# Soft mixture of experts behind attention: the experts' outputs combined as fp32 products on four row groups

## The chip, the cores and the metric

The kernel runs on one core of one Trainium2 chip. A core has five engines that run side by side and wait for each other through semaphores: TensorE (PE in the profile, with its weight loads as PEld), VectorE (DVE), ScalarE (ACT), GpSimd (POOL) and SyncE (SP), which here issues the transfers between DRAM and the on-chip memory SBUF. Products of TensorE land in PSUM, eight banks of 2 KB per partition, and are copied from there to SBUF by ACT or DVE. The metric is the device time of one execution in microseconds; less is better.

## The reference, cut to what matters

Attention with a memory term gives `x` of 4608 rows and 512 columns (eight batches of 576 rows). The change touches what is done with `x` last:

```python
logits = x @ phi                                  # 4608 x 32: 8 experts, 4 slots each
d = exp(logits - max over rows); d /= d.sum(0)    # dispatch
slot_input = (d.T @ x).reshape(8, 4, 512)
for e in range(8):
    slot_out[e] = relu(slot_input[e] @ w1[e]) @ w2[e]
c = exp(logits - max over slots); c /= c.sum(1)   # combine weights
return c @ slot_out                               # 4608 x 32 times 32 x 512
```

## The kernel before

The program has two parts. The first, up to about 464 us, walks over 32 pairs of heads (eight batches, four pairs) and computes attention. As blocks of 512 rows of `x` (nine blocks, `NQ`) are finished, it accumulates the dispatch and prepares the combine weights of blocks 0 to 6. The order of its operations is written out by hand as a list of names (`SEQ`), and a function `pin` ties every instruction to its predecessor on the same engine, so each engine runs in the order of the code. In this part the first 44 of 64 weight tiles of the experts (512 KB each) are loaded by SP into free places of SBUF (`wload`; `wslot` notes the place of each). The change does not touch it.

The second part, from about 464 us on, is the code after `pl.release()`:

- `f1(eg, f)`: first expert layer for a group of four experts and half of the hidden units, as products on four column groups of 32 (one expert each), then relu on ACT. `f1t` transposes the result through PSUM; DVE copies it to `hT`.
- `f2(dh, eg, f)`: second layer for half `dh` of the 512 output columns, also on four column groups. Its sum over `eg` and `f` is in `po[dh]`.
- `c1`, `c2`: the combine weights of blocks 7 and 8, and their transposes, into `cT`. In `cT` partition 32 j + s holds slot s for the j-th run of 128 rows of a block, for j from 0 to 3.
- `reload`: the 20 weight tiles not yet loaded go into the places of tiles that `f1` has read. SP issues them one after another.
- `c3(i, j)`: for each j, from the 32 rows of `cT`, a tile of 96 rows in the reduced type fp32r: the rounded weights, the remainder, and the rounded weights again. Two casts on ACT (`act`, line 355), one subtraction on DVE (line 984). `i` is 0 for blocks 0 to 7 and 1 for block 8.
- `g1(dh)` scales the experts' outputs by the dispatch's denominator on DVE (line 991). `g2(dh)` sums and spreads them to all partitions by a product with the constant `sel` (line 995), and splits them in the same way as the weights: `so` holds the rounded outputs in rows 0 to 63 and the remainder in rows 64 to 95.
- `comb(dh, t4)`: four products of 96 rows, one for each j (line 1006). Their three blocks of rows add up rounded times rounded, remainder times rounded, and rounded times remainder. Two j share a PSUM tile; ACT copies the first pair and DVE the second to SBUF, and SP issues the transfer of 512 x 256 numbers to the output (line 1008).

At the end stands the order: all of `f1`, `c1`, `c2`, `c3` and `f2` for the first half of the columns, `g1(0)`, a quarter of a step of `f2(1, 0, 0)`, `g2(0)`, the rest of that step, five `comb(0, ...)`, `f2(1, 0, 1)`, four more `comb(0, ...)`, the rest of `f2` for the second half, `g1(1)`, `g2(1)`, nine `comb(1, ...)`.

PSUM in this part: `psF` has two buffers of one bank for `f1` and `f2`, `psP` two for `f1t`, `c1`, `c2` and `g2`, `psC` four for `comb`.

Of the kernel before, what the change touches and what calls it, by code (L numbers as in the profile page):

```python
# [8 lines left out]
F32 = mybir.dt.float32  # L9
F32R = mybir.dt.float32r  # L10
AF = mybir.ActivationFunctionType
ALU = mybir.AluOpType
AX = mybir.AxisListType
PSUM = bass.MemoryType.PSUM
# [268 lines left out]
def tile_attn_soft_moe(ctx, tc, q, k, v, M, beta, phi, w1, w2, cst, out):  # L283
    nc = tc.nc
# [8 lines left out]
    cT = const.tile([128, NQ, 128], F32, name="cT")  # L293
# [29 lines left out]
    par = [ctx.enter_context(tc.tile_pool(name=f"par{i}", bufs=1)) for i in range(2)]  # L323
# [30 lines left out]
    def act(o, i):  # L354
        nc.scalar.copy(o, i)  # L355
# [385 lines left out]
    wt, wslot = {}, {}  # L741
# [169 lines left out]
    nw = len(WORD)  # L911
# [4 lines left out]


    psF = ctx.enter_context(tc.tile_pool(name="psF", bufs=2, space=PSUM, reuse_waits="tile"))
    psP = ctx.enter_context(tc.tile_pool(name="psP", bufs=2, space=PSUM, reuse_waits="tile"))
    psC = ctx.enter_context(tc.tile_pool(name="psC", bufs=4, space=PSUM, reuse_waits="tile"))  # L920
    reload = [wslot[order[x]] for x in [*range(8), *range(12, 4 + len(order) - nw)]]
    stage = [wslot[order[x]] for x in range(4 + len(order) - nw, 42)]
    cslot = [wslot[order[x]] for x in range(8, 12)]
    hT = rest[:, 0:2048].rearrange("a (e x y) -> a e x y", e=2, x=8)
    hs, po, cc = {}, {}, {}

# [8 lines left out]
        nc.scalar.activation(h, ps, AF.Relu)  # L935

    def f1t(eg, f):
        pt = psP.tile([128, 512], F32, name="pp")
        for x in range(4):
            nc.tensor.transpose(out=pt[:, 128 * x:128 * x + 128], in_=hs[eg, f][:, 128 * x:128 * x + 128], identity=ident)  # L940
        dve(hT[:, eg, 4 * f:4 * f + 4, :].rearrange("a x y -> a (x y)"), pt)
# [9 lines left out]


    def c1(qd):
        ps = psP.tile([128, 512], F32, name="pp")
        nc.tensor.transpose(out=ps[:, 0:128], in_=y["lt"][:, qd - 7, :], identity=ident)
        lk = ps[:, 0:128].rearrange("a (j s) -> a j s", s=32)
        m4 = sml.tile([128, 4], F32, name="m4")
        nc.vector.reduce_max(out=m4, in_=lk, axis=AX.X)
        c = cc[qd] = sml.tile([128, 4, 32], F32, name=("lt", "ex")[qd - 7], bufs=1)
        nc.vector.tensor_tensor(out=c, in0=lk, in1=m4.rearrange("a (j x) -> a j x", x=1).broadcast_to([128, 4, 32]), op=ALU.subtract)  # L960
        nc.scalar.activation(c, c, AF.Exp)
        s4 = sml.tile([128, 4], F32, name="s4")
        nc.vector.reduce_sum(out=s4, in_=c, axis=AX.X)
        nc.vector.tensor_scalar(out=s4, in0=s4, scalar1=1e-9, scalar2=None, op0=ALU.add)
        nc.vector.reciprocal(out=s4, in_=s4)
        nc.vector.tensor_tensor(out=c, in0=c, in1=s4.rearrange("a (j x) -> a j x", x=1).broadcast_to([128, 4, 32]), op=ALU.mult)

    def c2(qd):
        ps = psP.tile([128, 512], F32, name="pp")
        nc.tensor.transpose(out=ps[:, 0:128], in_=cc[qd].rearrange("a j s -> a (j s)"), identity=ident)  # L970
        act(cT[:, qd, :], ps[:, 0:128])


    cst4, cst8 = [], xkp.tile([128, 4, 128], F32R, name="xk")

    def c3(i, j):
        r = slice(32 * j, 32 * j + 32)
        if i == 0:
            pool, name = cslot[j]
            cst4.append(pool.tile([128, 8, 128], F32R, name=name))  # L980
        o, w = ((cst4[j], cT[r, 0:8]), (cst8[:, j], cT[r, 8]))[i]
        act(o[0:32], w)
        act(o[64:96], w)
        nc.vector.tensor_tensor(out=o[32:64], in0=w, in1=o[64:96].bitcast(F32), op=ALU.subtract)


    so = par[0].tile([128, 2, 256], F32R, name="k")
    ogs = par[1].tile([128, 2, 256], F32, name="k")

    def g1(dh):  # L990
        nc.vector.tensor_scalar(out=ogs[:, dh], in0=po[dh][:, 0:256], scalar1=dt, scalar2=None, op0=ALU.mult)

    def g2(dh):
        pm = psP.tile([128, 512], F32, name="pp")
        nc.tensor.matmul(pm[:, 0:256], sel, ogs[:, dh], start=True, stop=True)
        act(so[0:96, dh], pm[0:96, 0:256])
        nc.vector.tensor_tensor(out=so[64:96, dh], in0=pm[64:96, 0:256], in1=so[64:96, dh].bitcast(F32), op=ALU.subtract)

    def comb(dh, t4):
        pool, name = stage[NQ * dh + t4]  # L1000
        o = pool.tile([128, 4, 256], F32, name=name)
        for half in range(2):
            ps = psC.tile([128, 2, 256], F32, name="pc")
            for v2 in range(2):
                u = 2 * half + v2
                nc.tensor.matmul(ps[:, v2], (cst4[u][0:96, t4, :] if t4 < 8 else cst8[0:96, u, :]), so[0:96, dh], start=True, stop=True)  # L1006
            (act, dve)[half](o[:, 2 * half:2 * half + 2, :], ps)
        nc.sync.dma_start(out=out[512 * t4:512 * t4 + 512, 256 * dh:256 * dh + 256].rearrange("(u a) d -> a u d", a=128), in_=o)

    f1(0, 0)  # L1010
# [7 lines left out]
    c2(8)  # L1018
    f1(1, 1)
    f1t(1, 0)  # L1020
    c3(0, 0)
    f2(0, 0, 0)
    f1t(1, 1)
    for x, (pool, name) in enumerate(reload):
        wload(nw + x, pool, name)
    for j in range(1, 4):
        c3(0, j)
    for j in range(4):
        c3(1, j)
    f2(0, 0, 1)  # L1030
    f2(0, 1, 0)
    f2(0, 1, 1)
# [79 lines left out]
```

## Time and profile before

| what | us |
|---|---|
| median of 3 runs (lowest to highest) | 531.93 (530.93 to 534.14) |
| span of the profiled execution | 529.8 |
| TensorE busy | 462.5 (87%) |
| DVE busy | 384.3 (73%) |
| ACT busy | 342.4 (65%) |
| SP's transfers on the 16 DMA engines | 61.6% of their time |

The profile is of one execution; its span runs from the first to the last instruction, and no device time is given for that execution beside the span. The shares are averages over the whole program. In the profile L12 is line 12 of the kernel; a row such as `pf<-w,at` names the tile written and the tiles read, without buffer numbers. Many tiles of the second part carry the names of places that an earlier tile held (`w`, `xt`, `q`, `K`, `X`, `mv`, `rm`). An fp32 product shows as two records, an fp32r product and a transpose as one. In a row of the timeline the first number is the start in the span, the second the length from the start of the first to the end of the last of its records; in brackets stands the idle time before it and what ended that.

### The profile page before, as it was taken

What the parts mean: (1) busy time and instruction counts of PE and PEld (TensorE: products, weight loads), DVE (VectorE), ACT (ScalarE), POOL (GpSimd) and SP (SyncE); (2) the same over time, 40 slices, a digit from 0 to 9 for tenths busy, and PEclk for the clock granted to TensorE, in tenths of its full rate; (3) what the DMA queues carried; (4) which work ended last, traced back from release to release, by engine and by line L of the source; (5) the groups of instructions that cost most, each with busy time, mean ns of one, the idle gap of its engine ahead of it and who ended that gap; (6) DMA issues with size and microseconds to landing.
All of it is one profiled execution on the core that took longest, in us unless ns stands there. A gap on an engine that the chain in (4) does not pass through costs nothing.

```text
span 529.8 us, 11904 instructions
## 1 busy us (share of the span) xinstructions
PE 462.5 (87%) x3970; PEld 312.9 (59%) x3970; DVE 384.3 (73%) x1324; ACT 342.4 (65%) x985; POOL 126.0 (24%) x138
## 2 busy tenths in 40 slices
PE   8989889789998799899888897999998988989783
PEld 5656566556666566576555665766665655634462
DVE  6889788787697688879767878588886864534442
ACT  5777777666788477757767677676874864316432
POOL 4233122332213214235113332223324200000000
PEclk9999999999999999999989999899998989999795
DMA  5654655766465446554646565374564765999599
GB/s 198 178 143 132 191 158 150 209 191 188 142 200 146 137 136 171 143 147 128 188 123 171 185 182 162 83 233 117 158 203 125 218 196 168 379 415 408 222 337 323
DMA packets 66285, 101.78 MB, mean 192 GB/s; under 512 B 11248, under 2 KB 41520, under 8 KB 66224
## 3 DMA queue, kind: packets, MB, share of 16 engines
q1 hardware_dynamic: 65936, 100.93, 61.6%
q8 instruction: 32, 0.52, 0.4%
q14 instruction: 29, 0.24, 0.2%
q10 hardware_dynamic: 288, 0.09, 0.1%
HBM read 91.25 MB, written 9.73 MB: 191 GB/s over the span
## 4 chain that ended last, share of the span: by engine, by line
PE 36%; DMA 25%; DVE 21%; SPq 6%; ACT 5%; issue 4%; POOL 1%; DVEq 0%; POOLq 0%; ACTq 0%
PE oa L598 6%; PE psT L560 6%; DMA rb<-rd 5%; PE psS L433 5%; DVE q L462 4%; PE psS L427 4%; DMA rm<-rs 4%; DMA k<-in_k_dram 4%; DMA rd<-rq 3%; DVE zq L462 3%; PE pf L932 3%; DVE qp L550 3%; PE pc L1006 3%; PE psT L592 3%; DMA q<-in_M_dram 2%
## 5 line engine op out<-in xcount | busy, mean ns | idle before, releaser
L355 ACT COPY at<-psT 128x256 f32<-128x256 f32 (+1 forms) x202 | 86.5, 479 | 52.3 <-PE psT L560 49.1
L470 ACT ACTIVATE q<-q,nm 128x512 f32<-128x512 f32 (+2 forms) x160 | 97.6, 612 | 15.3 <-DVE nm L462 15.2
L598 PE MATMUL oa<-at,mv 128*64 128x320 f32 (+4 forms) x640 | 93.1, 427 | 3.0 <-DMA mv<-in_v_dram 1.3
L427 PE MATMUL psS<-k,qq 128*128 128x256 f32 (+2 forms) x320 | 69.2, 330 | 16.5 <-DVE nm L462 12.0
L462 DVE CUSTOM_DVE_ANT_0 q<-psS,mv 128x512 f32<-128x512 f32 (+1 forms) x128 | 76.1, 611 | 6.6 <-PE psS L433 3.9
L560 PE MATMUL psT<-cs,q 128*128 128x128 f32 x480 | 75.6, 282 | 2.8 <-DVE xt L633 1.1
L433 PE MATMUL psS<-K,X 64*128 64x512 f32 (+2 forms) x576 | 70.5, 365 | 8.5 <-DVE nm L462 6.1
L470 ACT ACTIVATE zq<-zq,nm 128x256 f32<-128x256 f32 (+2 forms) x128 | 67.7, 531 | 7.2 <-DVE nm L462 6.6
L427 PEld LDWEIGHTS psS<-k,qq 128*128 128x128 f32 x320 | 51.9, 199 | 28.3 <-DVE nm L462 17.6
L560 PEld LDWEIGHTS psT<-cs,q 128*128 128x128 f32 x480 | 58.0, 148 | 9.0 <-issue 2.3
L433 PEld LDWEIGHTS psS<-K,X 64*128 64x128 f32 x576 | 46.1, 188 | 26.9 <-issue 9.8
L598 PEld LDWEIGHTS oa<-at,mv 128*64 128x64 f32 x640 | 38.1, 137 | 38.0 <-issue 27.0
L560 PE MATMUL psT<-cs,zq 128*128 128x128 f32 x288 | 48.5, 283 | 2.3 <-DVE xt L633 0.9
L505 POOL TENSOR_SCALAR qp<-qq 128x576 f32<-128x576 f32 x19 | 31.8, 1676 | 74.0 <-PE psT L593 60.2
L550 DVE TENSOR_TENSOR qp<-qp,rb 128x576 f32<-128x576 f32 x32 | 27.0, 843 | 21.2 <-DMA rb<-rd 21.2
L626 DVE TENSOR_TENSOR xt<-oa,rm 128x448 f32<-128x448 f32 (+7 forms) x60 | 23.8, 435 | 24.2 <-DMA rm<-rs 18.1
L411 POOL TENSOR_TENSOR K<-k,K 128x512 fp32r<-128x512 f32 x25 | 32.8, 1314 | 31.3 <-ACT K L355 18.9
L358 DVE COPY at<-psT 128x512 f32<-128x512 f32 (+1 forms) x59 | 32.4, 570 | 10.1 <-PE psT L560 8.6
L592 PE MATMUL psT<-qp,q 128*128 128x512 f32 x64 | 35.1, 629 | 4.4 <-DVE qp L550 3.1
L560 PEld LDWEIGHTS psT<-cs,zq 128*128 128x128 f32 x288 | 34.8, 147 | 6.1 <-ACT at L355 1.1
L530 POOL TENSOR_TENSOR rn<-rn,rm 128x144 f32<-128x144 f32 x22 | 10.5, 477 | 91.3 <-ACT rn L523 57.9
L470 ACT ACTIVATION_READ_ACCUMULATOR q<-q,nm 128x1 f32 x160 | 31.0, 193 | 0.0
(214 smaller groups left out, 760.7 us busy)
## 6 DMA issues: line engine op xcount, KB each, us to landing
w<-in_w_dram SPq DMA_DIRECT2D x49, 512.0 KB
qq<-in_q_dram SPq DMA_DIRECT2D x32, 480.0 KB
mv<-in_v_dram SPq DMA_DIRECT2D x64, 160.0 KB
k<-in_k_dram SPq DMA_DIRECT2D x32, 288.0 KB
rb<-rd SPq DMA_DIRECT2D x64, 144.0 KB
rm<-rs SPq DMA_DIRECT2D x64, 144.0 KB
q<-in_M_dram SPq DMA_DIRECT2D x32, 80.0 KB
out_dram<-w SPq DMA_DIRECT2D x5, 512.0 KB
```

The source lines that it names most:

```text
L355: nc.scalar.copy(o, i)
L358: nc.vector.tensor_copy(out=o, in_=i)
L411: ALU_ENG[ev("kl", n)].tensor_tensor(out=K2[:, 1, :], in0=st[n]["k"][:, 0:512], in1=K2[:, 0, :].bitcast(F32), op=ALU.subtract)
L427: nc.tensor.matmul(ps[:, c + x0 - k0:c + x1 - k0], s["qd"][:, i], s["k"][:, x0:x1], start=True, stop=True)
L433: nc.tensor.matmul(ps[:, c0:c0 + N], X[ROW[h], x, 128 * i - 128:128 * i], K2[ROW[h], y, 0:N], start=(x, y) == (0, 0), stop=(x, y) == (0, 1))
L462: nc.vector.tensor_tensor_reduce(out=sm, in0=src, in1=msk, op0=ALU.add, op1=ALU.min, scale=-0.125, scalar=m0, accum_out=acc_o)
L470: nc.scalar.activation(sm, sm, AF.Exp, scale=-1.0, bias=s["nm"][:, J:J + 1], accum_out=s["sum"][:, J:J + 1])
L505: ALU_ENG[ev("qmin", n)].tensor_scalar(out=st[n]["qp"], in0=st[n]["q"], scalar1=0.0, scalar2=None, op0=ALU.min)
L550: ALU_ENG[ev("qn", n)].tensor_tensor(out=s["qp"], in0=s["qp"], in1=s["rb"], op=ALU.mult)
L560: nc.tensor.transpose(out=ps[:, 128 * x:128 * x + 128], in_=src[:, k0:k0 + 128], identity=ident)
L592: nc.tensor.matmul(om, s["m"][:, 0:128], s["qp"][:, 64:576], start=True, stop=True)
L598: nc.tensor.matmul(o[ROW[h], col:col + nx], vt[:, c, ROW[h]], at[:, a0 + hs * h:a0 + hs * h + nx], start=start, stop=stop)
```

## The change

`c3` and its tiles are gone. The combine takes `cT` as it is: half `half` and index `v2` of a pair pick the 32 rows of `cT` for j = 2 half + v2, and the product is of fp32 with the same 32 rows of `so`, which now holds the experts' outputs unsplit in all four groups of 32 partitions. The two products of a pair write to two PSUM banks; `psC` is gone, and `psP` has three buffers of two banks each, which `comb` shares with `f1t`, `c1`, `c2` and `g2`. The four places that `c3` took (those of tiles 8 to 11) take reloads, and the list of reloads ends with place 19 instead of 23.

```diff
-    psP = ctx.enter_context(tc.tile_pool(name="psP", bufs=2, space=PSUM, reuse_waits="tile"))
-    psC = ctx.enter_context(tc.tile_pool(name="psC", bufs=4, space=PSUM, reuse_waits="tile"))
-    reload = [wslot[order[x]] for x in [*range(8), *range(12, 4 + len(order) - nw)]]
-    stage = [wslot[order[x]] for x in range(4 + len(order) - nw, 42)]
-    cslot = [wslot[order[x]] for x in range(8, 12)]
+    psP = ctx.enter_context(tc.tile_pool(name="psP", bufs=3, space=PSUM, reuse_waits="tile"))
+    reload = [wslot[order[x]] for x in range(len(order) - nw)]
+    stage = [wslot[order[x]] for x in range(24, 42)]
...
-        ps = psP.tile([128, 512], F32, name="pp")
+        ps = psP.tile([128, 2, 512], F32, name="pp")[:, 0]
...
-    cst4, cst8 = [], xkp.tile([128, 4, 128], F32R, name="xk")
-
-    def c3(i, j):
-        r = slice(32 * j, 32 * j + 32)
-        if i == 0:
-            pool, name = cslot[j]
-            cst4.append(pool.tile([128, 8, 128], F32R, name=name))
-        o, w = ((cst4[j], cT[r, 0:8]), (cst8[:, j], cT[r, 8]))[i]
-        act(o[0:32], w)
-        act(o[64:96], w)
-        nc.vector.tensor_tensor(out=o[32:64], in0=w, in1=o[64:96].bitcast(F32), op=ALU.subtract)
...
-    so = par[0].tile([128, 2, 256], F32R, name="k")
+    so = par[0].tile([128, 2, 256], F32, name="k")
...
-        act(so[0:96, dh], pm[0:96, 0:256])
-        nc.vector.tensor_tensor(out=so[64:96, dh], in0=pm[64:96, 0:256], in1=so[64:96, dh].bitcast(F32), op=ALU.subtract)
+        act(so[:, dh], pm[:, 0:256])
...
-            ps = psC.tile([128, 2, 256], F32, name="pc")
+            ps = psP.tile([128, 2, 512], F32, name="pp")
             for v2 in range(2):
-                u = 2 * half + v2
-                nc.tensor.matmul(ps[:, v2], (cst4[u][0:96, t4, :] if t4 < 8 else cst8[0:96, u, :]), so[0:96, dh], start=True, stop=True)
-            (act, dve)[half](o[:, 2 * half:2 * half + 2, :], ps)
+                r = slice(64 * half + 32 * v2, 64 * half + 32 * v2 + 32)
+                nc.tensor.matmul(ps[:, v2, 0:256], cT[r, t4, :], so[r, dh], start=True, stop=True)
+            (act, dve)[half](o[:, 2 * half:2 * half + 2, :], ps[:, :, 0:256])
...
-    for j in range(1, 4):
-        c3(0, j)
-    for j in range(4):
-        c3(1, j)
```

What stands in a row on DVE between the last copies of `f1t` and the first copies of `comb(0, ...)`, before (`w_6132` to `w_6207` and `xk` are the split weights, `k` the tiles of `g1` and `g2`):

```order
L984 TENSOR_TENSOR w_6132<-cT,w_6132 32x1024
L358 COPY at<-pp 128x512
L984 TENSOR_TENSOR w_6199<-cT,w_6199 32x1024
L984 TENSOR_TENSOR w_6203<-cT,w_6203 32x1024
L984 TENSOR_TENSOR w_6207<-cT,w_6207 32x1024
L984 TENSOR_TENSOR xk<-cT,xk 32x128 x4
L991 TENSOR_SCALAR k<-pf,dt 128x256
L997 TENSOR_TENSOR k<-pp,k 32x256
L358 COPY w_6293<-pc 128x512
```

And now:

```order
L358 COPY at<-pp 128x512 x3
L976 TENSOR_SCALAR k<-pf,dt 128x256
L358 COPY w_6260<-pp 128x512
L358 COPY w_6270<-pp 128x512
L358 COPY K_6280<-pp 128x512
```

Between the last transpose's copy and `g1` no instruction is left, and none between `g1` and the first copy of an output. ACT, at the same place, before:

```order
L355 CAST w_6132<-cT 32x1024 x2
L355 CAST w_6199<-cT 32x1024 x2
L355 CAST w_6203<-cT 32x1024 x2
L355 CAST w_6207<-cT 32x1024 x2
L355 CAST xk<-cT 32x128 x8
L355 CAST k<-pp 96x256
L355 COPY w_6293<-pc 128x512
```

And now:

```order
L355 COPY cT<-pp 128x128 x2
L933 ACTIVATE qp<-pf 128x512
L355 COPY k<-pp 128x256
L355 COPY w_6260<-pp 128x512
L355 COPY w_6270<-pp 128x512
```

The sixteen casts are gone, and the copy of `g2` stands right behind the last relu. On TensorE the number and the order of the products stay. SP's reloads, before (the name after DMA is the place):

```order
L752 DMA w6_6171<-in_w2_dram 128x1024
L752 DMA w7_6173<-in_w2_dram 128x1024
L752 DMA w12_6175<-in_w2_dram 128x1024
L752 DMA w13_6177<-in_w2_dram 128x1024
L752 DMA w14_6179<-in_w2_dram 128x1024
```

And now:

```order
L752 DMA w6_6163<-in_w2_dram 128x1024
L752 DMA w7_6165<-in_w2_dram 128x1024
L752 DMA w8_6167<-in_w2_dram 128x1024
L752 DMA w9_6169<-in_w2_dram 128x1024
L752 DMA w10_6171<-in_w2_dram 128x1024
```

From the ninth reload on each goes to a place that is four lower.

More of the change, by code (lines that the diff above doesn't have):

```diff
@@ L937, in f1t @@
     def f1t(eg, f):
-        pt = psP.tile([128, 512], F32, name="pp")
+        pt = psP.tile([128, 2, 512], F32, name="pp")[:, 0]
         for x in range(4):
@@ L968, in c2 @@
     def c2(qd):
-        ps = psP.tile([128, 512], F32, name="pp")
+        ps = psP.tile([128, 2, 512], F32, name="pp")[:, 0]
         nc.tensor.transpose(out=ps[:, 0:128], in_=cc[qd].rearrange("a j s -> a (j s)"), identity=ident)
         act(cT[:, qd, :], ps[:, 0:128])
-    cst4, cst8 = [], xkp.tile([128, 4, 128], F32R, name="xk")
-    def c3(i, j):
-        r = slice(32 * j, 32 * j + 32)
-        if i == 0:
-            pool, name = cslot[j]
-            cst4.append(pool.tile([128, 8, 128], F32R, name=name))
-        o, w = ((cst4[j], cT[r, 0:8]), (cst8[:, j], cT[r, 8]))[i]
-        act(o[0:32], w)
-        act(o[64:96], w)
-        nc.vector.tensor_tensor(out=o[32:64], in0=w, in1=o[64:96].bitcast(F32), op=ALU.subtract)
-    so = par[0].tile([128, 2, 256], F32R, name="k")
+    so = par[0].tile([128, 2, 256], F32, name="k")
     ogs = par[1].tile([128, 2, 256], F32, name="k")
@@ L993, in g2 @@
     def g2(dh):
-        pm = psP.tile([128, 512], F32, name="pp")
+        pm = psP.tile([128, 2, 512], F32, name="pp")[:, 0]
         nc.tensor.matmul(pm[:, 0:256], sel, ogs[:, dh], start=True, stop=True)
-        act(so[0:96, dh], pm[0:96, 0:256])
-        nc.vector.tensor_tensor(out=so[64:96, dh], in0=pm[64:96, 0:256], in1=so[64:96, dh].bitcast(F32), op=ALU.subtract)
+        act(so[:, dh], pm[:, 0:256])
     def comb(dh, t4):
@@ L1020, in tile_attn_soft_moe @@
     f1t(1, 0)
-    c3(0, 0)
     f2(0, 0, 0)
```

## The prediction

> **What bounds the kernel now.** I read the page for the shares, then the stages of the tail (the change touches nothing earlier), then the chain of waits in the tail, then SP's own rows. First the busy time by stages; the columns are stage, length, busy time of each engine, granted TensorE clock, DMA share, GB/s:
> ```profile
> 464.60:490.30 25.70, 24.63 (x280) 10.65 (x284) 9.40 (x20) 10.99 (x16) 0.00 (x0) 1.00 1.03 413
> 490.30:495.50 5.20, 1.53 (x10) 0.50 (x2) 2.82 (x6) 3.06 (x9) 0.00 (x0) 0.81 0.96 383
> 495.50:501.00 5.50, 5.50 (x39) 3.64 (x38) 1.74 (x4) 1.86 (x4) 0.00 (x0) 0.56 0.06 24
> 501.00:510.60 9.60, 9.24 (x119) 5.83 (x118) 4.62 (x8) 3.57 (x7) 0.00 (x0) 1.00 1.00 337
> 510.60:514.00 3.40, 1.93 (x11) 1.36 (x11) 1.36 (x3) 1.06 (x3) 0.00 (x0) 1.00 1.05 350
> 514.00:516.00 2.00, 2.00 (x9) 1.88 (x10) 1.52 (x3) 1.36 (x3) 0.00 (x0) 0.50 0.83 282
> 516.00:525.00 9.00, 4.88 (x21) 4.35 (x20) 4.15 (x6) 3.12 (x6) 0.00 (x0) 0.50 1.08 378
> 525.00:528.20 3.20, 0.00 (x0) 0.00 (x0) 0.00 (x0) 0.00 (x0) 0.00 (x0) 0.50 0.98 333
> ```
> The DMA engines are full with weight reads until 495.5, nearly idle (24 GB/s) until 501.0, and full with the output until 528.2; only 514 to 516 dips. From 501.0 the output, not TensorE, sets the end. So the hole of 5.5 us is what the change can win, and the chain says who makes it:
> ```profile
> 482.65 0.93 ACT w L355
> ...
> 493.54 0.28 DVE xk L984
> 493.82 0.03 issue
> 493.85 0.49 DVE k L991
> 494.34 0.04 issue
> 494.39 1.22 PE pp L995 x2
> 495.61 2.72 PE pf L949 x24
> 498.33 2.33 PE pc L1006 x10
> ```
> From 482.65 on it is the splitting of the combine weights (c3: ACT's L355 into w and xk, DVE's L984), then g1 (L991), which stands behind c3 on DVE, g2 (L995), a rest of f2 (L949), the first combine (L1006). The same steps ahead of the second combine, and SP's first issue of output:
> ```profile
> 511.15 0.71 PE pp L995 x2
> ...
> 511.89 0.38 ACT k L355
> ...
> 512.77 8.13 PE pc L1006 x36
> ```
> ```profile
> 500.27 1.24 SPq L1008 DMA_DIRECT2D out_dram<-w  x2
> ```
> An issue at 500.27 moves data at 501.0: 0.73 us.
>
> **The change, part by part.** c3 goes:
> ```profile
> L355 ACT CAST w<-cT 32x1024 fp32r<-32x1024 f32 x8 | 8.3, 1041 | 0.1
> L355 ACT CAST xk<-cT 32x128 fp32r<-32x128 f32 x8 | 2.4, 295 | 0.1
> ```
> ```profile
> L984 DVE TENSOR_TENSOR w<-cT,w 32x1024 fp32r<-32x1024 f32 x4 | 4.9, 1215 | 3.4 <-ACT w L355 3.4
> L984 DVE TENSOR_TENSOR xk<-cT,xk 32x128 fp32r<-32x128 f32 x4 | 1.1, 281 | 0.4
> ```
> 10.7 us of ACT and 6.0 of DVE. What is late next is f2(0), ahead of g1 on TensorE:
> ```profile
> 482.69 0.38 PE L949 MATMUL pf<-qq,at 128*32 128x256 f32 x1
> ...
> 482.90 0.38 PE L949 MATMUL pf<-qq,at 128*32 128x256 f32 x1
> ...
> 488.38 2.34 PE L949 MATMUL pf<-w,at 128*32 128x256 f32 x40
> ```
> Four column groups start a round together, a round is 0.216 us and its results are there 0.38 after its start (0.17 past the round); an fp32 product takes two rounds. Of the 40 records 32 (eight rounds) belong to f2(0): the last starts at 488.38 + 7 x 0.216 = 489.89 and ends at 490.27.
>
> The third buffer of psP takes away two waits ahead of that:
> ```profile
> 473.08 0.33 PE L955 MATMUL pp<-cs,rb 128*128 128x128 f32 x1 [0.68 <-DVE at L358]
> ```
> ```profile
> 478.03 0.33 PE L970 MATMUL pp<-cs,ex 128*128 128x128 f32 x1 [0.36 <-ACT cT L355]
> ```
> With three in rotation each finds its buffer free. Bounds 0 and 1.04 us; I take 1.04, since TensorE has no other gap there (24.63 busy of 25.70). f2(0) then ends at 489.23. The weights for it and for f2(1) are earlier: 512 KB at 413 GB/s are 1.27 us, the twenty reloads end at 495.5, so the eighth lands at 480.3.
>
> g1 then ends at 489.23 + 0.04 + 0.48 = 489.75, g2's product (0.71 at full clock) at 490.50, ACT's copy at 490.92; DVE's subtraction (L997) is gone. The rest of f2(1,0,0), six rounds at full clock instead of 2.72 us at half, ends at 490.50 + 1.30 = 491.8. The first combine starts there instead of 498.3.
>
> The new products: per tile of 512 rows four of fp32, two rounds each, on four row groups. The trace has no fp32 product on 32 rows. Bounds: all four side by side, 2 x 0.216 = 0.43 us a tile; one after another, 1.73. Before, it was 8.13/9 = 0.90 at half clock, so the one end is a gain and the other a loss on TensorE. The nearest row is that of two row groups of 64:
> ```profile
> L433 PEld LDWEIGHTS psS<-K,X 64*128 64x128 f32 x12 | 1.0, 184 | 1.2 <-DVE nm L462 1.2
> ```
> ```profile
> 303.58 1.49 PE L433 MATMUL psS<-K,X 64*128 64x384 f32 x12 [0.98 <-DVE nm L462]
> ```
> Twelve loads of 0.184 are 2.2 us, yet they are busy for 1.0: the two row groups load side by side, and all twelve products fit into 1.49. I take 0.43.
>
> The Trainium skill, "TensorE: Matmul & The Clock Gate", section "Part 3: Packing small matmuls — row/col tiling", says that a weight load overlaps running products only in another row group; within one, load and product would alternate. By these rows each group's six loads would take 1.1 us and leave 0.39 of the 1.49 for six products, 0.07 each, a third of a round: the trace disagrees. By that rule a buffer would be held for 2 x (0.186 + 0.216) + 0.89 = 1.69, a tile cost 1.13 at full clock, still under the output's pace, and the sum would stand; at half clock it would not, which is rival B.
>
> With products that short the buffers pace the combine:
> ```profile
> L358 DVE COPY w<-pc 128x512 f32<-128x512 f32 x5 | 3.5, 692 | 4.2 <-PE pc L1006 4.2
> ```
> ```profile
> L355 ACT COPY w<-pc 128x512 f32<-128x512 f32 x5 | 2.9, 587 | 4.5 <-PE pc L1006 4.4
> ```
> A buffer is held for 0.43 + 0.17 + 0.04 + 0.64 (mean of the copies) + 0.04 = 1.32 us; three give a half each 0.44, a tile each 0.88. The output needs 524 KB at 378 GB/s = 1.39 us a tile: hidden, with the copies; without that cover it would cost 18 x 0.88 = 15.8. g2's and f1t's use of the same pool adds no wait, their slots being read out by then.
>
> First output: 491.8 + 0.22 + 0.60 + 0.04 + 0.69 = 493.3. SP issues it behind the last reload, whose data end at 495.5, so output flows from 495.5 instead of 501.0. The reloads now take slots 8 to 11 instead of 20 to 23: freed earlier, but the queue is full anyhow, so nothing either way. The work ahead of 464.6 is untouched.
>
> Second combine: first ten halves 9 x 0.44 + 0.43, to 496.2; f2 eight rounds, 497.9; eight halves, 501.4; sixteen rounds and 0.17, 505.1; g1, g2 and copy 1.65, 506.7; first tile 1.55, issue at 508.3, data at 509.0. Until then nine tiles have to last: before, 9.6 x 337 + 3.4 x 350 = 4425 of 4719 KB by 514.0, the rest in 0.84 at 350: 13.8 us, here until 509.3. Covered with 0.3 us to spare; every later us costs itself.
>
> Sum: the 9.44 MB took 501.0 to 528.2, 27.2 us, of which the dip cost 2.0 x (350 - 282)/350 = 0.4. Without it 495.5 + 26.8 = 522.3, and 1.6 after the last data (528.2 to 529.8 before): 523.9, which is 5.9 below the profiled 529.8. The median of the runs is 531.93, 2.1 above the profiled span; I carry the difference: **526.0**. Bounds: all output at 378 GB/s, 25.0 us, gives 524.2; all at 337 gives 527.2, and a second combine late by 0.8 makes that 528.0.
>
> **The rivals.** (B) The second combine runs at half clock and becomes TensorE's. Rows for half clock (the smaller numbers are at full):
> ```profile
> L995 PEld LDWEIGHTS pp<-k,cs x4: 186/238/333, 494.4 to 511.3; 128*128 128x128 f32 x4
> L995 PE MATMUL pp<-k,cs x4: 379/558/794, 494.4 to 511.5; 128*128 128x256 f32 x4
> ```
> A round doubles to 0.43, results 0.37 later. Side by side a buffer holds 0.85 + 0.37 + 0.72 = 1.94, a tile 1.29: still under 1.39. If load and product of one group alternate, 2 x (0.33 + 0.43) + 0.37 + 0.72 = 2.61, a tile 1.74, nine 15.7: 506.7 + 15.7 = 522.4, plus 0.73 + 1.39 + 1.6 = 526.1, time 528.2. For it: 514 to 525 stood at 0.50 after the pause around g2. Against it: L433. This is also what the skill's rule would give.
>
> (C) The clock falls already in the first combine. 491.8 + 5 x 1.29 + 3.46 + 4 x 1.29 + 6.9 + 2.5 for g1, g2 and copy + 2.4 for a tile = 518.7; data at 519.4, 13.2 us for nine tiles, 1.6: 534.2, time 536.3. For it: the clock fell at 514 and stayed down although TensorE was busy for 2.00 of 2.00 us. Against it: 501.0 to 510.6 stood at 1.00 with products and f2 mixed as here.
>
> (D) Row groups of 32 do not overlap in fp32: 1.73 a tile. The end is then 503.4 + 18P (491.8, f2 5.4, g1 to copy 1.65, last half and landing 4.6), P being a tile's products; above P = 1.47 the kernel is slower than before. 1.73 gives 534.5, time 536.7; with half clock in the second combine 550.1, time 552. For it: no such row exists. Against it: L433's two groups.
>
> **How the numbers follow.** Forecast 0.67, B 0.14, C 0.08, D 0.11. A measurement of this kernel can tell about 1% (5.3 us) from no change: faster than 526.6, slower than 537.3. The forecast's 526.0 lies just beyond, so of its 0.67 I give 0.47 to faster; the rest with B, C and half of D is within 1% (0.47); D with half clock is 0.06. The range goes from the forecast's lower bound, 524.0, past B to no change, 532.0, since a partial overlap puts P anywhere below 1.47; it leaves out C and D, 0.19.
>
> **What would show it.** Right: the copies into fp32r are gone, L976 (g1) starts near 489.3 and the first L992 issue near 493.3; GB/s never falls near zero between 495 and 522; L990's eight products of a tile take under 0.9 us. Wrong: L976 waits on something else than f2; a hole in the DMA rate before the tenth output (B, C); L990 records in single file (D); an output that flows at another rate than 337 to 378 moves the end without TensorE.

## The result, and the profile after

| | before | changed |
|---|---|---|
| median of 20 executions each (lowest to highest), us | 533.89 (529.47 to 541.53) | 531.39 (522.95 to 539.61) |
| ratio changed to before | | 0.987 (95% interval 0.983 to 0.991) |
| span of the profiled execution, us | 529.8 | 529.8 |

The changed kernel is faster by 1.3%, between 0.9 and 1.7%. On the 531.93 us of the prediction that is 525.0 us; 526.0 had been predicted. The ratio is formed from executions in which nothing disturbed the core, so it is not the quotient of the two medians, and the profiled execution of the changed kernel is not one of them.

That execution shows why two equal spans say nothing here. The chain of waits shows where the second part begins, first of before, then of the changed kernel (start, length, engine, tile, line, number of records; rows of "issue" are left out):

```profile
464.64 7.07 PE pf L932 x64
```

```profile
469.69 7.07 PE pf L930 x64
...
488.99 5.36 PE pf L947 x96
494.38 0.50 DVE k L976
494.92 0.70 PE pp L980 x2
495.62 1.43 PE pf L947 x24
497.05 0.66 PE pp L990 x8
497.73 0.59 ACT w L355
498.36 0.73 PE pp L990 x6
499.11 0.70 DVE w L358
499.86 0.72 PE pp L990 x7
...
511.04 0.49 DVE k L976
...
512.73 0.72 PE pp L990 x8
```

The first product of `f1` stands at 464.64 before and at 469.69 now: the part that the change does not touch took 5.05 us longer in this execution. From there to the end it is 529.8 - 464.6 = 65.2 us before and 60.1 now, 5.06 less by the unrounded times. All readings below are therefore from the first product of `f1` on; the stretch from there to the end of the span is called the tail.

The page's busy times follow the code: ACT has 331.8 us (342.4 before), DVE 378.0 (384.3), TensorE 461.3 (462.5).

```profile
PE 461.3 (87%) x4042; PEld 307.6 (58%) x4042; DVE 378.0 (71%) x1314; ACT 331.8 (63%) x969; POOL 124.5 (23%) x138
```

In the chain the splits of the weights are gone: ahead of `g1` (L976) stands `f2` (L947) alone. `g1` starts 24.69 after `f1`, before it was 29.21; the first combine (L990) follows 2.6 later, before 4.4. The busy time by stages, in the columns of the prediction's first view:

```profile
469.69:494.30 24.61, 24.36 (x280) 10.62 (x284) 5.63 (x17) 3.54 (x8) 0.00 (x0) 1.00 1.02 411
494.30:499.30 5.00, 4.57 (x60) 2.44 (x50) 1.36 (x3) 1.47 (x4) 0.00 (x0) 1.00 0.98 391
499.30:512.30 13.00, 11.42 (x150) 6.00 (x146) 5.64 (x9) 3.98 (x7) 0.00 (x0) 1.00 1.02 350
512.30:515.00 2.70, 2.01 (x24) 1.46 (x24) 0.82 (x2) 1.45 (x3) 0.00 (x0) 1.00 0.33 114
515.00:528.10 13.10, 5.56 (x52) 2.86 (x48) 5.17 (x8) 4.09 (x7) 0.00 (x0) 0.78 1.04 360
```

The hole of 5.5 us at 24 GB/s between the last reload and the first output is closed: 391 GB/s and then 350. The clock stays at 1.00 through both combines (the 0.78 of the last row is the time after 522, when TensorE has done). But a new hole has opened, 2.7 us at 114 GB/s. SP's rows show what the transfers wait for there, first of the changed kernel, then the tenth issue of before:

```profile
498.54 1.72 SPq L992 DMA_DIRECT2D out_dram<-w  x2
...
508.48 1.21 SPq L992 DMA_DIRECT2D out_dram<-qq  x1
514.29 0.37 SPq L992 DMA_DIRECT2D out_dram<-w  x1
```

```profile
514.30 0.37 SPq L1008 DMA_DIRECT2D out_dram<-w  x1
```

The ninth issue is at 508.48, the tenth, which is the first of the second combine, at 514.29. By 513.2 (43.5 after `f1`) 99% of the nine tiles are written, and the queue runs dry until the tenth. So the first output goes out 6.8 us sooner than before (28.85 after `f1` instead of 35.64), and the tenth 5.06 sooner (44.60 instead of 49.66). The end follows the tenth: 15.53 behind its issue in both kernels.

### The profile page after: what moved, and what is told of

The parts are those of the page before. It is cut to its first block, busy times and chain, and to the rows that moved or that the text cites. A ratio compares the mean times of both kernels' runs of the same rounds, so it can differ in the third digit from the quotient of the medians.

```text
span 529.8 us, 12019 instructions
## 1 busy us (share of the span) xinstructions
PE 461.3 (87%) x4042; PEld 307.6 (58%) x4042; DVE 378.0 (71%) x1314; ACT 331.8 (63%) x969; POOL 124.5 (23%) x138
## 4 chain that ended last, share of the span: by engine, by line
PE 34%; DMA 24%; DVE 24%; SPq 6%; ACT 4%; issue 4%; POOL 1%; DVEq 0%; POOLq 0%; ACTq 0%
DMA rm<-rs 9%; PE psT L560 6%; DVE q L462 5%; PE psS L427 5%; PE oa L598 4%; PE psS L433 4%; DVE zq L462 3%; DMA q<-in_M_dram 3%; DMA rs<-rts 3%; DMA k<-in_k_dram 3%; PE pf L947 3%; PE pf L930 2%; DVE at L358 2%; PE psT L592 2%; PE pp L990 2%
## 5 line engine op out<-in xcount | busy, mean ns | idle before, releaser
L427 PE MATMUL psS<-k,qq 128*128 128x256 f32 (+2 forms) x320 | 67.7, 324 | 15.3 <-DVE nm L462 12.6
L427 PEld LDWEIGHTS psS<-k,qq 128*128 128x128 f32 x320 | 50.8, 195 | 27.2 <-DVE nm L462 18.2
```

The source lines that it names most:

```text
L427: nc.tensor.matmul(ps[:, c + x0 - k0:c + x1 - k0], s["qd"][:, i], s["k"][:, x0:x1], start=True, stop=True)
```

## The experiments

**What was to be told apart.** The theory is that of the prediction: the gain is the hole, it closes because the splits are off the path to `g1`, with shares for the third buffer and for a clock that no longer falls; then the output's rate sets the end as long as the second combine is ready in time. The rivals: the fast products on four row groups are what counts (D of the prediction, if they do not run side by side); the clock is what counts; the second combine is what sets the end, and with it the way in which `f2` is spread among the first combine.

All positions follow from each profile in one way: the start of the row in question less the start of the first product of `f1` (for the changed kernel 494.38 - 469.69 = 24.69). `g1`, combine, outputs and end are in us after `f1`; the last column is the ratio of the times to before, with its interval.

| run | `f1` starts | `g1` | first combine | first output | tenth output | end (tail) | ratio |
|---|---|---|---|---|---|---|---|
| before | 464.64 | 29.21 | 33.62 | 35.64 | 49.66 | 65.19 | 1 |
| changed | 469.69 | 24.69 | 27.29 | 28.85 | 44.60 | 60.13 | 0.987 (0.983 to 0.991) |
| e1_again | 473.89 | 24.69 | 27.29 | 28.85 | 44.60 | 60.13 | 0.990 (0.986 to 0.995) |
| e11_again5 | 469.80 | 24.69 | 27.29 | 28.85 | 44.61 | 60.13 | 0.992 (0.987 to 0.996) |
| e10_before_again | 469.22 | 30.90 * | 35.31 | 37.33 | 51.45 | 66.88 | |
| e2_splits_kept | 472.17 | 29.87 * | 33.72 | 35.68 | 51.43 | 66.63 | 1.002 (0.997 to 1.007) |
| e3_one_group | 468.06 | 24.68 | 27.29 | 30.07 | 65.96 | 97.15 | 1.058 (1.050 to 1.067) |
| e4_spread | 466.70 | 26.38 * | 28.98 | 30.54 | 44.39 | 60.54 | 0.991 (0.987 to 0.995) |
| e5_before_third_buffer | 467.04 | 28.19 | 32.41 | 33.95 | 48.94 | 64.12 | 0.998 (0.994 to 1.002) |
| e6_before_warm | 464.99 | 29.21 | 31.81 | 33.34 | 47.23 | 62.89 | 0.995 (0.991 to 0.999) |
| e7_moved | 475.17 | 24.69 | 27.29 | 28.85 | 43.40 | 60.40 | 0.988 (0.982 to 0.994) |
| e8_two_buffers | 467.68 | 25.71 | 28.32 | 29.88 | 54.52 | 73.64 | 1.021 (1.015 to 1.026) |
| e9_three_places | 468.91 | 24.69 | 27.29 | 28.85 | 43.69 | 59.63 | 0.994 (0.990 to 0.998) |
| e12_rounded | 470.02 | 26.38 * | 28.98 | 30.51 | 45.01 | 60.57 | 0.980 (0.973 to 0.987) |

In the four rows with a star the clock was halved for 3.4 us at the start of `f1`, which puts everything behind it 1.69 us later; e10_before_again shows it.

**e1_again, e11_again5: the changed kernel twice more, and e10_before_again: the kernel before once more.** No edit.

> The changed kernel once more, unchanged. What is looked at is the tail, from the first product of f1 to the end of the span: 65.2 us in the profile of before, 60.1 in that of after. Theory (the change acts in the tail alone, and its attention part varies from execution to execution): the tail is again 58.5 to 60.5 us, whatever the part ahead of it takes. Rival (the longer attention part of the profile of after, 5 us, comes from the change): that part is again longer than 468 us, and the tail is what it was.

> The changed kernel a third time, with more rounds. Theory (5.06 us less in the tail, nothing ahead of it): a ratio of 0.990 within its interval, a tail of 60.1 us. Rival (the attention part of the changed kernel is longer by some us): a ratio nearer to 1 than 0.995.

> The kernel before once more. Theory (the tail is fixed by the program, the attention part varies from execution to execution): the tail is 65.2 us within 0.5, and the part ahead of it is anywhere between 464 and 475. Rival (that part is the same in each execution of the same program): 464.6 within 0.5.

The tail of the changed kernel is 60.13 in all three profiles, and every position in it agrees to 0.02 us. So the gain of the tail is 65.19 - 60.13 = 5.06 us, which is 0.95% of 533.9. The three ratios, 0.987, 0.990 and 0.992, hold 0.9905 in their intervals.

The part ahead of `f1` is not so steady: 469.69, 473.89 and 469.80 here, 464.64 and 469.22 for the kernel before. The profile of e10_before_again shows beside this the halved clock. Its first 3.9 us of `f1`, and the same 3.9 us of before:

```profile
469.22:473.12 3.90, 3.90 (x24) 1.28 (x28) 0.12 (x1) 0.00 (x0) 0.00 (x0) 0.56 1.03 418
```

```profile
464.64:468.54 3.90, 3.90 (x39) 1.45 (x43) 0.12 (x1) 0.14 (x1) 0.00 (x0) 1.00 1.02 418
```

The granted clock is 0.56 and 24 records start instead of 39, at the same DMA rate and with the same code. `g1` is late by 30.90 - 29.21 = 1.69. This hits kernels of either kind (e10_before_again as much as e4_spread) and is not a matter of the change.

**e2_splits_kept: the splits put back into the changed kernel.** The tiles they write are read by nothing; the combine still takes `cT`.

```diff
+    cslot = [wslot[order[x]] for x in range(20, 24)]
+    def c3(i, j):
...
+        act(o[0:32], w)
+        act(o[64:96], w)
+        nc.vector.tensor_tensor(out=o[32:64], in0=w, in1=o[64:96].bitcast(F32), op=ALU.subtract)
...
+    for j in range(1, 4):
+        c3(0, j)
+    for j in range(4):
+        c3(1, j)
```

> The changed kernel with the sixteen casts and eight subtractions of c3 put back at their old places on ACT and DVE; their tiles lie in the places of weight tiles 20 to 23 and are read by nothing. Theory (the splits on ACT and DVE ahead of g1 are what held the output back): g1 starts 3 to 4 us later after the first product of f1 than in the changed kernel, near 28 us instead of 24.7, TensorE waits long enough there for the granted clock to fall, and the tail grows by 3.5 to 5.5 us, to 63.5 to 65.5. Rival (what counts is the new products and the buffers of PSUM): the tail stays within 1 us of the changed kernel's.

The gain is gone (ratio 1.002). Less the 1.69 of the halved clock `g1` is at 28.18, 3.5 later than in the changed kernel, and the tail 64.9. Its chain of waits has the picture of before again:

```profile
501.73 0.28 DVE xk L983
...
502.05 0.49 DVE k L990
...
502.58 0.70 PE pp L994 x2
503.28 2.68 PE pf L947 x24
505.96 1.05 PE pp L1004 x8
```

`g1` (here L990) starts when the last subtraction ends, and the rest of `f2` takes 2.68 us instead of 1.43, since the clock has fallen during the wait (0.79 in the mean of 500.17 to 508.17). With the splits back on the path, the new products and the third buffer together leave 65.19 - 64.94 = 0.25 us of the tail's gain: the splits, not the form of the products, are what cost. The run also keeps the new places of the reloads, so these are not what gained.

**e5_before_third_buffer: the third buffer alone, in the kernel before.** `psC` gives up a bank for it.

```diff
-    psP = ctx.enter_context(tc.tile_pool(name="psP", bufs=2, space=PSUM, reuse_waits="tile"))
-    psC = ctx.enter_context(tc.tile_pool(name="psC", bufs=4, space=PSUM, reuse_waits="tile"))
+    psP = ctx.enter_context(tc.tile_pool(name="psP", bufs=3, space=PSUM, reuse_waits="tile"))
+    psC = ctx.enter_context(tc.tile_pool(name="psC", bufs=3, space=PSUM, reuse_waits="tile"))
```

> The kernel before with psP at three buffers instead of two, and psC at three instead of four. Theory (two waits of TensorE for a buffer of psP, 0.68 and 0.36 us, lie ahead of f2(0), and the splits start behind the last relu, which comes that much earlier): g1 starts 1.0 us earlier after the first product of f1 (28.2 instead of 29.2), the first output likewise, and the tail is 64.0 to 64.8 us instead of 65.2. Rival (the splits hide that gain): g1 stays at 29.2. A second look is at the part ahead of f1, which this edit does not touch either: if it too varies by several us from 464.6, the longer one in the profiles of the changed kernel says nothing of the change.

`g1` starts at 28.19 instead of 29.21, 1.02 sooner (1.04 was the prediction's term), and the tail is 1.07 shorter: 0.2%, which the ratio of 0.998 allows but does not show. The splits move forward with the transposes, so this share is there even while they remain.

**e6_before_warm: seven filler products in the kernel before**, between `g1` and `g2`, so that TensorE does not pause there. Nothing reads them.

```diff
+    fill = psC.tile([128, 2, 256], F32, name="pc")
+    for x in range(7):
+        nc.tensor.matmul(fill[:, x % 2], sel, hT[:, 0, 0:2].rearrange("a x y -> a (x y)"), start=True, stop=True)
```

> The kernel before with seven more fp32 products of 128 rows on TensorE between f2(1, 0, 0)'s first step and g2(0), whose results are read by nothing: they fill 3 us of the wait for g1. Theory (part of what the splits cost is that TensorE waits so long that its granted clock falls): g1 starts as before, near 29.2 after the first product of f1, the clock stays at 1.00, the way from g1 to the first combine shrinks from 4.4 us to 2.6 to 3.1, and the first output is issued 1.3 to 1.9 us earlier. Rival (the way from g1 to the combine is long for another reason): it stays above 4 us.

Its stage around `g1`, then its chain:

```profile
494.00:502.00 8.00, 7.44 (x80) 4.58 (x78) 4.34 (x8) 3.18 (x6) 0.00 (x0) 1.00 0.51 180
```

```profile
494.20 0.49 DVE k L991
...
494.74 0.70 PE pp L995 x2
495.44 1.43 PE pf L949 x24
496.88 1.63 PE pc L1006 x10
```

The clock stays at 1.00. `g1` is where it was (29.21), but `g2` and the rest of `f2` take 0.70 and 1.43, as in the changed kernel, where before had 1.22 and 2.72. The combine starts 1.81 sooner. The first output is issued 2.30 sooner, more than the 1.3 to 1.9 expected, because the chain's first combine is shorter too (1.63, before 2.33), and the tail is 2.30 shorter (0.4%, ratio 0.995). So a part of what the splits cost was not their own time but the clock that their wait let fall, and a few products without use win that part back.

With e2, e5 and e6 the 33.62 - 27.29 = 6.33 us by which the first combine starts sooner come apart: 3.5 the wait of `g1` for the splits, 1.02 the third buffer, 1.81 the clock between `g1` and the combine. Their sum is 6.33.

**e3_one_group: all four products of a tile on the same row group.** All then multiply the first 32 rows of `cT`, so the output repeats one run of 128 rows four times.

```diff
-                r = slice(64 * half + 32 * v2, 64 * half + 32 * v2 + 32)
+                r = slice(0, 32)
```

> The changed kernel with all four products of a tile on the first row group, so the output repeats the first 128 rows of each 512 in the other three. Theory (the four row groups work side by side, and this is what keeps fp32 products off the path): here they run one after another, a tile takes 1.7 us or more on TensorE instead of 0.95, and the tail grows to between 69 and 72 us, slower than before. Rival (the pace of the combine is that of the copies and buffers, whatever the groups do): a tile stays under 1.1 us and the tail within 1 us of the changed kernel's.

Two stages of its first combine:

```profile
495.30:500.40 5.10, 5.10 (x27) 4.36 (x24) 1.38 (x2) 1.61 (x3) 0.00 (x0) 1.00 0.97 375
500.40:507.40 7.00, 7.00 (x18) 5.29 (x16) 1.38 (x2) 1.32 (x3) 0.00 (x0) 0.50 0.68 238
```

24 loads (three tiles of eight records) take 5.1 us, 1.70 a tile, and from 500.4 on, at a clock of 0.50, 16 take 7.0, 3.5 a tile. The first number is the 1.73 that rival D priced; so products in one group do run one after another, and in the changed kernel they do not. The second was in no expectation: TensorE was busy for 5.10 of 5.10 us when the clock fell. The tail of 97.15, where 69 to 72 was expected, is mostly this.

**e8_two_buffers: two buffers for the combine instead of three,** and two of one bank for the transposes, `c1`, `c2` and `g2`.

```diff
-    psP = ctx.enter_context(tc.tile_pool(name="psP", bufs=3, space=PSUM, reuse_waits="tile"))
+    psP = ctx.enter_context(tc.tile_pool(name="psP", bufs=2, space=PSUM, reuse_waits="tile"))
+    psC = ctx.enter_context(tc.tile_pool(name="psC", bufs=2, space=PSUM, reuse_waits="tile"))
...
-            ps = psP.tile([128, 2, 512], F32, name="pp")
+            ps = psC.tile([128, 2, 512], F32, name="pc")
```

> The changed kernel with the pool for the combine apart from that for the transposes, as two buffers of two banks, and the other with two of one bank as before. Theory (a buffer of the combine is held for 1.4 us, and buffers over that time set its pace): a tile takes 1.4 us instead of 0.96, g1 comes 1.0 us later, the tenth output 5 us later than in the changed kernel, near 49.5 us after the first product of f1, and the tail is 64 to 66 us, which is that of the kernel before. Rival (TensorE's products or the copies pace the combine): a tile stays under 1.1 us, and the tail grows by about 1 us.

TensorE's timeline and the two stages that it falls into:

```profile
495.99 0.71 PE L991 MATMUL pc<-k,cT 32*128 32x256 f32 x8
497.38 0.87 PE L991 MATMUL pc<-k,cT 32*128 32x256 f32 x8 [0.67 <-ACT w L355]
...
500.15 1.61 PE L991 MATMUL pc<-k,cT 32*128 32x256 f32 x8 [0.41 <-ACT K L355]
```

```profile
495.90:500.00 4.10, 2.65 (x28) 1.35 (x24) 1.60 (x3) 1.66 (x3) 0.00 (x0) 1.00 0.74 267
500.00:507.00 7.00, 6.58 (x48) 3.27 (x48) 1.86 (x3) 1.27 (x3) 0.00 (x0) 0.51 0.88 304
```

A tile now waits for the copies (0.67 us in the brackets) and starts 1.39 us after the one before it (495.99, then 497.38), where 1.4 was expected. After 4 us of that, with TensorE busy for 2.65 of 4.10, the clock falls to a half, and a tile takes 2.0 (issues at 32.87, 34.88, 36.90). The tail is 13.5 us longer than in the changed kernel, where 4 to 6 were expected. The clock is that of rival C, here with pauses between the products; why it fell is not shown.

**e4_spread: the rest of `f2` in small pieces**, two of its twelve steps behind each of the combines 0 to 5, `g1(1)` behind the seventh and `g2(1)` behind the eighth.

```diff
+    rest2 = [(1, *x, (c,)) for x in ((0, 1), (1, 0), (1, 1)) for c in range(4)]
     for t4 in range(NQ):
         comb(0, t4)
-        if t4 == 4:
-            f2(1, 0, 1)
-    f2(1, 1, 0)
-    f2(1, 1, 1)
-    g1(1)
-    g2(1)
+        for x in rest2[2 * t4:2 * t4 + 2]:
+            f2(*x)
+        if t4 == 6:
+            g1(1)
+        if t4 == 7:
+            g2(1)
```

> The changed kernel with the last twelve steps of f2 for the second half of the columns placed two by two behind the first six combines of the first half, g1(1) behind the seventh and g2(1) behind the eighth. Theory (behind the first nine outputs the queue runs dry because TensorE waits for buffers in the combine and does f2 afterwards): f2 fills those waits, the second combine starts 3 to 5 us earlier, the hole in the output goes, and the tail is 1 to 3 us shorter than the changed kernel's, 57 to 59. Rival (the output's own rate sets the end): the tail changes by less than 0.5 us.

The hole is gone, but the tail is not shorter: 60.54 where 57 to 59 was expected, or 58.9 if the 1.69 of the halved clock could be taken off in full. Less the 1.69 the tenth output is issued at 42.70, 1.9 sooner than in the changed kernel. The output starts 1.7 us later than the changed kernel's, as late as the halved clock makes it, and runs without a break. In time nothing is to be seen (0.991 against 0.990 for e1_again in the same batch). TensorE's timeline shows the price:

```profile
495.68 0.71 PE L990 MATMUL pp<-k,cT 32*128 32x256 f32 x8
496.32 1.07 PE L947 MATMUL pf<-w,at 128*32 128x256 f32 x16
497.32 0.71 PE L990 MATMUL pp<-k,cT 32*128 32x256 f32 x8
```

A combine and two steps are two rounds and four; at 0.216 that would be 1.30 us, and the next combine starts 1.64 later (1.645 between the issues of the first seven outputs, in the mean): 0.35 are lost with each change from row groups to column groups and back. TensorE waits for no other engine there. The Trainium skill, "TensorEngine Tiling (Array Packing)", section "Key Properties", says that changing the tiling mode drains TensorE. The records of this trace part the 0.35: at either change the next load starts 0.32 or 0.33 behind the start of the last round instead of 0.216, 0.22 for the pair, which fits that rule; the other 0.13 are the first loads of a combine (0.10) and of a step (0.02), which their products wait for.

**e7_moved and e9_three_places: the rest of `f2` sooner, in whole steps.** e7_moved puts `f2(1, 0, 1)` behind the third combine, the other two steps and `g1(1)` behind the fifth, `g2(1)` behind the seventh; e9_three_places gives each of the three steps a place of its own.

```diff
+        if t4 == 2:
+            f2(1, 0, 1)
         if t4 == 4:
-            f2(1, 0, 1)
-    f2(1, 1, 0)
-    f2(1, 1, 1)
-    g1(1)
-    g2(1)
+            f2(1, 1, 0)
+        if t4 == 6:
+            f2(1, 1, 1)
+            g1(1)
+        if t4 == 7:
+            g2(1)
```

(The diff is that of e9_three_places.)

> The changed kernel with f2(1, 0, 1) behind the third combine instead of the fifth, f2(1, 1, 0), f2(1, 1, 1) and g1(1) behind the fifth instead of the ninth, and g2(1) behind the seventh. Theory (the end is set by when the tenth output is ready, and the wait for g1 and its copy can be covered by the last combines of the first half; no more switches between f2 and combine than before): the tenth output is issued at 43.5 to 44.0 us after the first product of f1 instead of 44.6, and the tail is 59.0 to 59.6 instead of 60.13. Rival (the first outputs then come too late and the output runs dry earlier): the tail is 60 or more.

> The changed kernel with f2(1, 0, 1) behind the third combine of the first half, f2(1, 1, 0) behind the fifth, f2(1, 1, 1) and g1(1) behind the seventh, and g2(1) behind the eighth: the same three blocks of f2, but one block at a time. Theory (outputs must come at least as fast as the transfers take them, 1.4 to 1.5 us each, at every place): the sixth output is issued near 37 us after the first product of f1 and the tenth near 43.4, the transfers run without a hole from 31 on, and the tail is 58.2 to 59.4 us, 0.7 to 1.9 below the changed kernel's 60.13. Rival (a later hole takes the place): 60 or more.

In e7_moved the hole only moves, since sixteen rounds of `f2` in one piece hold back the sixth output, and the tail is 60.40 where 59.0 to 59.6 was expected:

```profile
512.00:515.00 3.00, 2.75 (x30) 1.32 (x22) 1.60 (x3) 1.07 (x2) 0.00 (x0) 1.00 0.35 120
```

In e9_three_places one microsecond of it is left (the eighth output is issued at 40.98, and about 80 KB move in the microsecond behind that); the tail is 59.63, 0.5 shorter than the changed kernel's and 0.2 above the expected 58.2 to 59.4. In time it is not seen: 0.994 beside 0.992 for the changed kernel in the same batch. So the tenth output can come 0.9 to 1.2 sooner, and no more than 0.5 of that reaches the end.

**e12_rounded: one fp32r product of 96 rows for each run of 128 rows**, as in the kernel before, but straight from `cT` and `so` in fp32r, into three buffers of one bank that the combine has to itself. It leaves out the remainders of both factors, and every run takes the same 96 rows; only its time is of use.

```diff
-    cT = const.tile([128, NQ, 128], F32, name="cT")
+    cT = const.tile([128, NQ, 128], F32R, name="cT")
...
+    psC = ctx.enter_context(tc.tile_pool(name="psC", bufs=3, space=PSUM, reuse_waits="tile"))
...
-    so = par[0].tile([128, 2, 256], F32, name="k")
+    so = par[0].tile([128, 2, 256], F32R, name="k")
...
-            ps = psP.tile([128, 2, 512], F32, name="pp")
+            ps = psC.tile([128, 2, 256], F32, name="pc")
...
-                nc.tensor.matmul(ps[:, v2, 0:256], cT[r, t4, :], so[r, dh], start=True, stop=True)
+                nc.tensor.matmul(ps[:, v2], cT[0:96, t4, :], so[0:96, dh], start=True, stop=True)
...
```

> The changed kernel with the weights and outputs rounded to fp32r, one fp32r product of 96 rows for each of the four runs of 128 rows in place of an fp32 product of 32, all four reading the same 96 rows, and three buffers of one bank: it leaves out the remainders of the splits and the choice of the rows, so its output is not the reference's. It shows what the form of the product costs when no splits stand ahead. Theory (the fp32 products on four groups hold a buffer for 0.70 us, fp32r ones for about 0.4): a tile takes 0.7 to 0.8 us instead of 0.96, the tenth output is issued 1.5 to 2.5 us earlier than at 44.6, and the tail is 58.2 to 59.5 us. Rival (the form of the products makes no difference, since buffers and copies pace both): the tenth output is issued within 0.5 us of 44.6.

TensorE's timeline of its first combine:

```profile
499.00 0.97 PE L990 MATMUL pc<-k,cT 96*128 96x256 f32 x6
500.18 1.07 PE L990 MATMUL pc<-k,cT 96*128 96x256 f32 x6 [0.20 <-ACT w L355]
```

Six records are a tile and a half, three buffers; they come round after 1.18 us, in the changed kernel after 1.38. From `g1` to the tenth output it takes 45.01 - 26.38 = 18.63, there 19.92: 1.29 less, where 1.5 to 2.5 had been expected. That is what the form of the products, mainly the second round of an fp32 product, costs the readiness of the second combine. The tail, with the halved clock in it, is 60.57. The ratio of 0.980 is lower than this tail explains (4.62 us are 0.9%, with the 1.69 of the halved clock 1.2%; the interval ends at 0.987), and what else was shorter in the timed executions the profile does not show.

## Why the prediction was right, and where it was not

**The hole and its causes: right.** All three shares came as worked out. `g1` starts at 24.69 after `f1`, and the prediction has it behind the end of `f2(0)` and an issue, 489.27 - 464.64 = 24.63. The third buffer is worth 1.02 (1.04). `g2` and the rest of `f2` run at full clock (2.60 from `g1` to the combine; 2.53 by the forecast). The combine starts at 27.29, 27.16 was said; the first issue at 28.85, 28.66 was said. e2_splits_kept shows that the splits are the cause, and e6_before_warm that the clock's share is a share of its own.

**Rivals B, C and D: wrong for this kernel.** L990 runs on four groups side by side, eight records in 0.66 to 0.73 us, and the clock stays at 1.00 to the end of the second combine. The row of two groups of 64 pointed the right way, but it bore less than the prediction put on it. Its twelve products are of fp32r, one record each, six with 384 columns and six with 512, so they say nothing of fp32 rounds; within one group they start 0.17 to 0.28 us apart. That groups work side by side was in the row; that four groups of 32 do so in fp32 was a guess, and it held.

The rivals are not far. e3_one_group runs at D's price when the groups are one, and in e8_two_buffers the clock falls in the first combine, as in C, with one buffer less. Half clock in the second combine alone, on the other hand, would have cost little: e2_splits_kept ran it at 0.50 (523.7 to 533.9) and issued a tile every 1.28 us, near the 1.29 that B has for groups side by side, and its end came 15.2 behind the tenth issue.

**The readiness of the second combine: the term that was mis-sized.** The prediction held a buffer for 0.43 + 0.17 ahead of the copy, 1.32 us in all, and had the tenth output issued at 508.3, which is 43.66 after `f1`, "covered with 0.3 us to spare". It is issued at 44.60. The chain above shows a buffer come round after 499.86 - 498.36 = 1.50 (with DVE's copy of 0.70) and 501.24 - 499.86 = 1.38 (with ACT's of 0.59), 1.44 in the mean. The copies, by their groups, are as in the rows quoted then:

```profile
L358 DVE COPY w<-pp 128x512 f32<-128x512 f32 x5 | 3.4, 689 | 5.8 <-PE pp L990 5.8
...
L355 ACT COPY w<-pp 128x512 f32<-128x512 f32 x5 | 2.8, 587 | 3.7 <-PE pp L990 3.7
```

The products are 0.72, not 0.60. The two forms of L990 in the first tile show why (duration in ns, least, median and most; first and last start):

```profile
L990 PEld LDWEIGHTS pp<-k,cT x8: 181/184/185, 497.0 to 497.1; 32*128 32x128 f32 x8
L990 PE MATMUL pp<-k,cT x4: 479/479/479, 497.0 to 497.0; 32*128 32x256 f32 x4
```

```profile
L990 PE MATMUL pp<-k,cT x4: 374/374/374, 497.5 to 497.7; 32*128 32x256 f32 x4
```

The first record behind a wait takes 479 ns, a later one 374. The first load starts with its product, at 497.0, and not ahead of it, so 105 ns of it are not hidden, and the second round starts 0.105 + 0.216 = 0.32 later. The same is to be seen inside the row of before that gave 1.49 for twelve products, once its first and its later products are taken apart:

```profile
L433 PE MATMUL psS<-K,X x2: 437/437/437, 303.6 to 303.6; 64*128 64x384 f32 x2
```

```profile
L433 PE MATMUL psS<-K,X x2: 332/332/333, 304.0 to 304.0; 64*128 64x384 f32 x2
```

437 against 332, again 105. It was read as one sum over twelve products, in which that disappears; but in the changed kernel 60 of the 72 products pay it in their first record (374 to 432 ns in the other twelve). Where a half of a tile waits for a copy, it does so for 0.25 us (ACT) or 0.31 (DVE).

The rule of the Trainium skill, "TensorE: Matmul & The Clock Gate", section "Part 3: Packing small matmuls — row/col tiling", that the prediction weighed there (a load overlaps running products only in another row group) does not fit either: the loads of the second round start at 497.1, under the products of the first round in the same group. By it a buffer came round after 1.69; measured are 1.44, between it and the 1.32 taken.

Where the 0.94 went: 0.13 at the first combine, 0.50 over its first ten halves (f2(1, 0, 1) starts at 501.88 - 469.69 = 32.19 instead of 31.56), some 0.2 over f2(1, 0, 1) itself and the other eight halves (the last `f2` starts at 507.31 - 469.69 = 37.62 instead of 36.76), and the rest in and behind the last `f2`.

**The output's flow: right in its rate, wrong in its shape.** 27 us without a break were predicted, from 495.5 - 464.64 = 30.86 after `f1` on, with the end at 59.26. By the records of the transfers the writes started at 29.8, since the reads had ended a microsecond sooner than in before, and 99% of the nine tiles were out 13.7 us later, at the predicted rate. So the queue was dry at about 43.5, 1.2 us sooner than worked out, while the tenth tile came a microsecond late: that is the hole of 2.7 us. In e1_again and e11_again5 the reads ended about a microsecond later and 99% of the nine tiles were out at 44.0, and the tail is the same 60.13. So half a microsecond more or less in the first nine tiles did not reach the end: the tenth output set it. The 6.8 us won at the first output, less what the hole costs (some 2 us of full rate, where before had lost 0.4 in its own dip), leave about the 5.06 of the tail. Forecast were 5.93, with the end at 59.26 instead of 60.13. e9_three_places, where little of the hole is left, ends at 59.63, so about 0.5 of the missing 0.87 is the hole's. The rest fits the rate: the whole output was taken at 26.8 us, and in e4_spread, where it has no break, it took 27.8 (31.5 to 59.3).

**The size: right.** 5.06 us are 0.95% of the time; the three ratios are 0.987, 0.990 and 0.992. The predicted 526.0 of 531.93 is 0.989.

**What stays open.** The part ahead of `f1`, with the same instructions in the same order, took 464.6 to 469.2 us in the four profiles of the kernel before and its two variants, and 466.7 to 475.2 in the others. The times show no such difference: had the changed kernel lost 4 us there, its ratio would be near 1. Whether the profiled executions are only few and scattered was not settled.

## What to carry to other kernels

Work that keeps the path waiting costs more than its own time if TensorE pauses for it: here 1.8 of 6.3 us were the clock, and seven products without use won them back. When a hole ahead of a stream closes, the next question is whether the stream's second half is ready earlier by as much; here it was not, by 1.7 us, and moving work forward only moved the hole. In a chain of waits price a product with its own weight load, if both wait for the same buffer.

## What the runs showed of the hardware

Four fp32 products on 32 rows each run fully side by side when they stand on four row groups (eight records in 0.66 us), and strictly one after another on one (1.70 us a tile at a clock of 1.00).

Changing between products on column groups and on row groups and back costs 0.35 us of TensorE in e4_spread, 0.22 of it at the two changes themselves.

The clock falls in ways that busy shares do not foretell. It fell in e8_two_buffers with TensorE busy for 2.65 of 4.10 us, and in e3_one_group with 5.10 of 5.10. In four of fourteen profiles it was halved for 3.4 us just at the start of `f1`, behind a stretch like this one of e10_before_again:

```profile
465.80:469.22 3.42, 2.75 (x42) 2.50 (x35) 2.03 (x11) 0.55 (x3) 0.00 (x0) 1.00 1.03 417
```

TensorE is busy for 2.75 of these 3.42 us, and in the changed kernel, whose clock did not fall there, just as much (2.72 of 3.39, from 466.30 on). The Trainium skill, "TensorE: Matmul & The Clock Gate", section "Part 1: The HAM clock gate (the "warmup" mystery)", has the clock fall after an idle window of about 3.4 us, on a window that runs on its own. The length agrees (0.56 over 3.9 us is 3.4 us at a half), and so does a window that runs on its own: in each of the fourteen traces the spells at half clock begin on a grid of 3.41 us that runs through the whole execution. Where a line of that grid lies 0.1 to 0.9 us behind the start of `f1`, the clock is halved from there (the four profiles); where the first line lies 1.3 to 3.1 us behind it, it is not (the ten others). So the position of the window separates them without exception. That a window must be idle does not agree: TensorE was 80% busy in the 3.41 us ahead of the fall in each of the four, and as busy in the window of the grid around the start of `f1` in nine of the ten others. What is counted as activity stays open.
